# Load order, gate and slice order at the head of a fused attention and gated feed-forward kernel

## The chip, the core and the metric

The kernel runs on one NeuronCore of a Trainium2 chip. The metric is the device time of one execution in microseconds (us). Before the change it is 227.95 us, the median of three runs (227.84 to 228.86).

The core's engines run side by side, each through its own list of instructions in order: TensorE (PE) multiplies matrices, VectorE (DVE), ScalarE (ACT) and GpSimd (POOL) do elementwise work, and SyncE (SP) mostly issues transfers. Sixteen DMA engines carry all transfers, whichever engine issued them. PE writes its results to PSUM, which has eight banks here named b0 to b7.

## The reference

For each of 8 batches and 8 heads there are 512 rows x (64 wide) and 32 state rows. Both sides attend to each other, and what comes out goes through a feed-forward layer with a ReLU gate.

```python
def _attn_ref(x, state):                      # x (8, 8, 512, 64), state (8, 8, 32, 64)
    scores = scale * np.matmul(x, state.transpose(0, 1, 3, 2))
    ...                                       # softmax over the 32 state rows -> a
    xread = np.matmul(a, state)
    scores2 = scale * np.matmul(state, x.transpose(0, 1, 3, 2))
    ...                                       # softmax over the 512 x rows -> a2
    sread = np.matmul(a2, x)
    return np.concatenate([xread, sread], axis=2)

def _moe_ref(x, w_gate, w_val, w_out):        # x (4352, 512), d_ff 1536
    gate = np.maximum(x @ w_gate, 0.0)
    val = x @ w_val
    return gate * val @ w_out
```

The kernel doesn't form `xread`. For each batch it multiplies the state with the weights first (U = state @ w, the "c" and "u" units below), and then the softmaxed scores with U (the "gv" units), so a gv unit needs both the batch's attention (`ANS`) and a slice of `U`.

## The kernel before

The parts that the change touches. `x_dma_cast` loads a batch of x through GpSimd's queue, casting from float32 to bfloat16 on the way; the loads of batch 0 go through the queues of SyncE and ScalarE in float32, in four pairs of heads.

```python
    def x_dma_cast(b, parts=1):

        cast_on_load.add(b)
        xb_alloc(b)
        v = xb[b].rearrange("p (h c d) -> p h c d", h=H, c=NC)
        for i in range(parts):
            hs = slice(H * i // parts, H * (i + 1) // parts)
            nc.gpsimd.dma_start(out=v[:, hs], in_=x[b, hs].rearrange("h (p c) d -> p h c d", c=NC))
        xb[b] = xb[b].rearrange("p (h c d) -> p c h d", h=H, c=NC)

    def w_dma(src, dst, lo, hi):
        nc.gpsimd.dma_start(out=dst[:, :, lo:hi],
                            in_=src.rearrange("(j p) f -> p j f", p=128)[:, :, lo:hi])

    def wo_dma(lo, hi):
        nc.gpsimd.dma_start(out=wo_sb[:, lo:hi],
                            in_=moe_w_out.rearrange("(f p) m -> p f m", p=128)[:, lo:hi])
...
    def state_conv(g, half, eng):
        dst, src, keep = st_b[:, g % 3, :, half], st_f[:, g], odd[:, half:half + 1]
        if eng == "act":
            nc.scalar.activation(out=dst, in_=src, func=AF.Copy, scale=keep)
        else:
            e = {"dve": nc.vector, "pool": nc.gpsimd}[eng]
            e.tensor_scalar(out=dst, in0=src, scalar1=keep, scalar2=None, op0=ALU.mult)

    def state_T(g):
        ps = held["st", g] = bank("stT_ps").bitcast(BF16)[:, 0:512]
        for i in range(4):
            nc.tensor.transpose(ps.rearrange("p (q i m) -> p q i m", i=4, m=8)[:, :, i],
                                st_b[:, g % 3, i].rearrange("p h d -> p (h d)"), id128)

    def state_out(g, eng):
        copy[eng](out=stT[:, 2 * g:2 * g + 2].rearrange("p b j m -> p (b j m)"), in_=held["st", g])

...
            for c in range(NC):
                for h2 in range(2):
                    nc.tensor.transpose(ps[64 * h2:64 * h2 + 64, c, j], xb[b][:, c, 4 * half + 2 * j + h2], id128)
...
    def att_sum(b, jp):
        e_v = by_pair(e_sn[b], jp).rearrange("p r (j n) -> p r j n", n=Ns)
        cs = small.tile([128, 2 * NC, 2], FP32, name="cs", tag="cs")
        nc.vector.reduce_sum(out=cs, in_=e_v, axis=AX.X)
        rc = held["rc", b, jp] = small.tile([128, 2 * NC, 2], FP32, name="rc", tag="rc")
        nc.vector.reciprocal(out=rc, in_=cs)

    def att_scale(b, jp, eng="dve"):
        e_v = by_pair(e_sn[b], jp).rearrange("p r (j n) -> p r j n", n=Ns)
        {"dve": nc.vector, "pool": nc.gpsimd}[eng].tensor_tensor(out=by_pair(a_sn[b], jp).rearrange("p r (j n) -> p r j n", n=Ns), in0=e_v,
                                in1=held["rc", b, jp].to_broadcast([128, 2 * NC, 2, Ns]), op=ALU.mult)
...
    def u_mm(dst, b, w, lo, n):

        wsb = (wg_sb, wv_sb)[w]
        for j in range(NJ):
            for parity in range(2):
                r = 64 * parity
                nc.tensor.matmul(dst[parity][32 * j:32 * j + 32], stT[r:r + 64, b, j, 32 * parity:32 * parity + 32],
                                 wsb[r:r + 64, j, lo:lo + n], start=True, stop=True)
...
    def gv(b, jf):
        if b not in hsb:
            hsb[b] = hpool.tile([128, NF, S], BF16, name="h_sb", tag="h_sb")
        held["gv", b, jf] = [bank("gv_ps"), bank("gv_ps")], hsb[b][:, jf], S
        for w in range(2):
            for kc in range(NK):
                gv_mm(held["gv", b, jf][0], b, jf, w, kc)
```

`state_conv` makes the state bfloat16 for the transpose (`state_T`). `att_scale` divides the exponentials by their sums; its engine is an argument. A c unit multiplies the state with a slice of both weights, 128 or 256 columns wide; a u unit with 512 columns of one weight. A gv unit is four matmuls of 512 columns.

The opening, in the order in which it is issued:

```python
    ctx.enter_context(tc.manual_schedule())
    nc.vector.memset(warm, 0.0)
    xf[0] = xin.tile([128, H, NC, D], FP32, name="xf", tag="xf")
    for eng, j in ((nc.sync, 0), (nc.scalar, None), (nc.sync, 2), (nc.scalar, 1), (nc.scalar, 3)):
        if j is None:
            state_dma(eng, 0, 2)
        else:
            src = x[0, 2 * j:2 * j + 2].rearrange("h (p c) d -> p h c d", c=NC)
            eng.dma_start(out=xf[0][:, 2 * j:2 * j + 2], in_=src)
    make_identity(nc, id128)
    x_dma_cast(1, 2)
    nc.scalar.activation(out=tiny, in_=nc.const_aps.tensor(0.0, (128, 1), FP32), func=AF.Exp)
    nc.vector.reduce_sum(out=odd, in_=id128.rearrange("p (a h m) -> p h a m", h=2, m=8), axis=AX.XY)
    nc.gpsimd.memset(xa[:, :, :, D:D + 1], 1.0)

    def w_load(lo, n):
        w_dma(moe_w_gate, wg_sb, lo, lo + n)
        w_dma(moe_w_val, wv_sb, lo, lo + n)

    def late_loads():
        x_dma_cast(2)
        state_dma(nc.gpsimd, 2, B)
        wo_dma(0, 6)
        wo_dma(6, NF)
        x_dma(3, (nc.gpsimd,))

    def x_next(b):
        x_conv(b, 0, "pool")
        x_conv(b, 1, "pool")
        x_trans_dma(b)

    warm_ps = psum.tile([128, 512], FP32, name="warm_ps", tag="b7")

    def spin(n, cols=512):
        for i in range(n):
            nc.tensor.matmul(warm_ps[:, 0:cols], warm[:, 0:128], warm[:, 0:cols], start=True, stop=True)
```

`spin` is filler: matmuls on zeros whose results nobody reads, which keep PE busy while it would wait. The program that follows is a list of words, each a step with its arguments; the digits after @ are PSUM banks. Each engine runs its own words in this order. The steps that count here: `xc` casts a head pair of batch 0, `xT` and `xT2` transpose x on PE, `xo` copies the transposes out, `stc`, `stT`, `sto` do the same for the state, `sc` are the scores, `ex` the exponentials, `nr` their sums, `nx` the scaling, `aT` and `ao` transpose the attention and copy it out, `c`/`co`, `u`/`uo`, `gv` with `re` (ReLU) and `mu` (product), `o`/`of` the output product, `sr`/`sn` the state's side, `xp` a padded copy of x, `xn` the cast of the next batch, `wd` and `ld` the loads.

```python
    program = """
    stc.0.0.dve stc.0.1.act xc.0.0.pool spin.30.128 xT.0.0@0 stT.0@1 xc.0.1.pool wd.0.128 wd.128.128 wd.256.256
    wd.512.256 wd.768.256 wd.1024.256 wd.1280.256 ld xo.0.0.act xc.0.2.dve sto.0.act spin.10.128 xT.0.1@2 xo.0.1.dve
    xc.0.3.act spin.11.128 sc.0.0@3 xT.0.3@4 ex.0.0 xT.0.2@5 xo.0.3.dve xo.0.2.act nr.0.0 spin.14.128 sc.0.1@0
    xT2.1.0@1 ex.0.1 nx.0.0 xo2.1.0.act nr.0.1 spin.7.128 xT2.1.1@2 xo2.1.1.act spin.4.128 sc.1.0@3 nx.0.1 spin.7.128
    c.0.0.128@45 ex.1.0 sc.1.1@0 co.0.0.128.0.dve aT.0.0@1 co.0.0.128.1.act aT.0.1@2 nr.1.0 ex.1.1 ao.0.1.act
    spin.9.128 c.0.128.128@34 ao.0.0.dve c.1.128.128@50 co.0.128.128.0.act nr.1.1 spin.5.128 gv.0.0@21
    co.0.128.128.1.act co.1.128.128.1.act co.1.128.128.0.act nx.1.0 re.0.0 c.1.0.128@34 gv.0.1@05 nx.1.1
    co.1.0.128.1.act co.1.0.128.0.act mu.0.0 re.0.1 c.0.256.256@24 co.0.256.256.1.act co.0.256.256.0.dve
    ...
    mu.1.1 re.1.5 gv.1.0@02 mu.1.5 re.1.0 c.0.1024.256@54 mu.1.0 gv.1.4@31 co.0.1024.256.0.act co.0.1024.256.1.act
    gv.1.6@02 re.1.4 re.1.6 mu.1.4 gv.0.8@54 mu.1.6 re.0.8 gv.0.9@30 mu.0.8 stc.1.0.pool re.0.9 c.0.1280.256@15
    stc.1.1.pool stc.2.0.pool stc.2.1.pool stc.3.0.pool stc.3.1.pool xp.0 xp.1 xn.3 c.0.768.256@24 mu.0.9
    co.0.1280.256.1.act xT2.2.0@3 co.0.768.256.1.act co.0.1280.256.0.dve xT2.2.1@0 co.0.768.256.0.act xo2.2.0.dve
    stT.1@5 gv.0.10@41 sto.1.act xo2.2.1.dve re.0.10 gv.0.11@23 mu.0.10 re.0.11 gv.1.7@50 mu.0.11 re.1.7 sc.2.0@4
    gv.0.6@12 mu.1.7 ex.2.0 re.0.6 nr.2.0 gv.0.7@35 re.0.7 mu.0.6 o.0.0@6 mu.0.7 c.1.1280.256@40 u.2.0.0@13 nx.2.0
    ...
    aT.2.1@1 aT.2.0@4 ao.2.1.dve u.2.1.0@25 u.2.1.512@03 ao.2.0.dve uo.2.1.0.1.act sr.1@1 uo.2.1.0.0.dve o.0.7
    uo.2.1.512.0.act sn.1 uo.2.1.512.1.dve gv.2.2@45 re.2.2 gv.1.11@20 mu.2.2 re.1.11 gv.2.1@13 mu.1.11 re.2.1
    gv.2.3@45 mu.2.1 re.2.3 o.0.8 mu.2.3 gv.2.0@20 of.0.2.act re.2.0 o.0.9@7 mu.2.0 sr.0@1 sn.0 xp.2 xp.3
    """
```

After the program, a loop with a fixed pattern goes on from unit (2, 4) to the last batch; the change leaves it as it is.

The softmax here doesn't subtract the row's maximum and nothing guards it: scores larger than these inputs give would overflow.

## Time and profile before

| | |
|---|---|
| Median time | 227.95 us |
| Span in the profile | 226.6 us, granted PE clock 1.00 |
| ACT busy, DVE busy, POOL busy | 55%, 58%, 22% |
| PE idle, 60 to 212 us | 1.29 us of 152 |
| PE idle, 15 to 60 us | 1.32 us of 45 |
| PE idle, after 212 us | 3.55 us |
| Slices of weight loads landed | 11.30 to 27.73 us |

How to read it: a line of the groups or of the instructions in order of time names an engine, the line of the kernel (L117), the operation, what it writes and reads (out<-in), the shape and the count. In the order of time the first two numbers are the start and the duration in us, and the brackets at the end give the idle time of the engine just before and what ended it. "<-DMA" means that the landing of that transfer ended the wait. In the groups the numbers after the bar are the busy time in us, the mean of one instruction in ns, and the idle time before them. In the view of DMA issues the last number is the time from issue to landing in us, and the number of KB is counted in what is written.

### The profile page before, as it was taken

How to read it: one execution, taken by the hardware profiler on the slowest of the kernel's cores; microseconds unless marked ns; L12 is line 12 of the kernel's file. 1: busy time of each engine (PE TensorE's matmuls, PEld its weight loads, DVE VectorE, ACT ScalarE, POOL GpSimd, SP SyncE). 2: the span in 40 equal slices, each digit the busy share in tenths (PEclk: the TensorE clock that was granted, in tenths of full speed). 3: DMA queues.
4: the chain of work that ended last, by engine and by line, in shares of the span. 5: the costliest groups of instructions: out<-in, count | busy, mean ns of one | idle time of the engine just before them, and what ended most of it. 6: DMA issues, size and time to landing. Idle time of an engine off the chain costs nothing.

```text
span 226.6 us, 4970 instructions
## 1 busy us (share of the span) xinstructions
PE 219.1 (97%) x2004; PEld 110.8 (49%) x2033; DVE 130.4 (58%) x228; ACT 125.1 (55%) x238; POOL 49.6 (22%) x54
## 2 busy tenths in 40 slices
PE   7999999999999999999999999999999999999994
PEld 7764354444444444444434444345443444666543
DVE  1588777976488547764776468656755343222100
ACT  4698886745475754664556555455655444322221
POOL 6975349500643060006000600000000000000000
PEclk9999999999999999999999999999999999999999
DMA  6999999180718911591139213611311111111132
GB/s 207 170 160 196 197 243 273 53 185 0 227 53 123 293 53 46 123 283 61 48 87 246 91 46 93 142 46 46 95 46 49 48 46 48 48 49 67 72 94 94
DMA packets 37816, 25.76 MB, mean 114 GB/s; under 512 B 18880, under 2 KB 33216, under 8 KB 37792
## 3 DMA queue, kind: packets, MB, share of 16 engines
q1 hardware_dynamic: 25184, 17.11, 27.1%
q0 software_dynamic: 11440, 7.21, 20.6%
q10 hardware_dynamic: 1168, 1.11, 1.7%
...
## 4 chain that ended last, share of the span: by engine, by line
PE 92%; DMA 3%; issue 1%; DVE 1%; ACT 1%; POOL 0%; ACTq 0%; DVEq 0%; POOLq 0%
PE o_ps L347 37%; PE gv_ps L310 37%; PE gv_ps L327 5%; PE up L285 4%; DMA xf<-in_x_dram 3%; PE sc_ps L206 2%; PE upc L285 1%; PE sr_ps L258 1%; PE warm_ps L424 1%; PE o_ps L373 1%; DVE h_sb L338 1%; PE xT_ps L192 1%; PE aT_ps L241 0%; POOL st_b L135 0%; PE srT_ps L271 0%
## 5 line engine op out<-in xcount | busy, mean ns | idle before, releaser
L310 PE MATMUL gv_ps<-ans,U 128*128 128x512 bf16 x365 | 95.4, 380 | 1.3 <-DVE sn L267 0.3
L347 PE MATMUL o_ps<-wo_sb,h_sb 128*128 128x512 bf16 x362 | 93.6, 379 | 0.9 <-issue 0.3
L338 DVE TENSOR_TENSOR h_sb<-gv_ps,g_sb 128x512 bf16<-128x512 f32 x96 | 65.0, 687 | 42.0 <-ACT g_sb L334 40.0
L334 ACT ACTIVATE g_sb<-gv_ps 128x512 bf16<-128x512 f32 (+1 forms) x108 | 63.0, 584 | 45.9 <-PE gv_ps L310 33.2
L347 PEld LDWEIGHTS <-h_sb 128*128 128x128 bf16 x372 | 36.1, 98 | 41.2 <-issue 0.5
L310 PEld LDWEIGHTS <-U 128*128 128x128 bf16 x384 | 34.9, 98 | 41.2 <-issue 4.5
L355 ACT COPY o_sb<-o_ps 128x512 f32<-128x512 f32 x31 | 18.1, 585 | 21.7 <-PE o_ps L347 21.7
L295 DVE CAST U<-up 128x512 bf16<-128x512 f32 x37 | 23.9, 685 | 5.6 <-PE up L285 5.5
L295 ACT CAST U<-up 128x512 bf16<-128x512 f32 x35 | 18.9, 593 | 10.5 <-PE up L285 10.5
L153 POOL CAST xb<-xf 128x1024 bf16<-128x1024 f32 (+1 forms) x12 | 11.8, 1007 | 52.2 <-DMA xf<-in_x_dram 41.9
L250 POOL COPY xa<-xb 128x2048 bf16<-128x2048 bf16 x8 | 15.0, 1894 | 17.1 <-issue 14.1
L219 DVE TENSOR_REDUCE cs<-e_sn 128x16 f32<-128x512 bf16 x16 | 10.9, 682 | 8.4 <-ACT e_sn L213 8.4
L338 DVE TENSOR_TENSOR hs_sb<-gv_ps,g_sb 128x256 bf16<-128x256 f32 x12 | 5.1, 425 | 15.3 <-PE gv_ps L327 10.5
L225 DVE TENSOR_TENSOR a_sn<-e_sn,rc 128x512 bf16<-128x512 bf16 x16 | 12.5, 784 | 0.4
L213 ACT ACTIVATE e_sn<-sc_ps 128x512 bf16<-128x512 f32 x16 | 9.6, 601 | 5.1 <-PE sc_ps L206 4.9
L305 ACT CAST U<-upc 128x512 bf16<-128x512 f32 (+1 forms) x21 | 9.9, 522 | 2.1 <-PE upc L285 1.9
L285 PEld LDWEIGHTS <-stT 64*32 64x32 bf16 x512 | 5.0, 89 | 10.8 <-issue 10.1
L424 PE MATMUL warm_ps<-hs_sb 128*128 128x128 bf16 x97 | 9.0, 258 | 1.2 <-DVE hs_sb L390 1.2
L424 PEld LDWEIGHTS <-hs_sb 128*128 128x128 bf16 x97 | 7.6, 119 | 1.5 <-DVE hs_sb L390 1.2
L206 PEld LDWEIGHTS <-xT 128*128 128x128 bf16 x128 | 5.7, 98 | 3.4 <-DVE xT L183 0.4
L285 PE MATMUL up<-wg_sb,stT 64*32 64x512 bf16 x144 | 7.4, 386 | 0.0
L327 PE MATMUL gv_ps<-br,wg_sb 128*128 128x256 bf16 x48 | 7.2, 273 | 0.1
...
## 6 DMA issues: line engine op xcount, KB each, us to landing
out_dram<-o_sb SPq DMA_DIRECT2D x31, 256.0 KB, 2.3
xf<-in_x_dram SPq DMA_DIRECT2D x4, 1024.0 KB, 6.5
...
wg_sb<-in_moe_w_gate_dram POOLq DMA_DIRECT2D x5, 256.0 KB, 9.1
wv_sb<-in_moe_w_val_dram POOLq DMA_DIRECT2D x5, 256.0 KB, 9.6
xf<-in_x_dram POOLq DMA_DIRECT2D x1, 1024.0 KB, 18.0
xf<-in_x_dram SPq DMA_DIRECT2D x2, 256.0 KB, 4.3
xf<-in_x_dram ACTq DMA_DIRECT2D x2, 256.0 KB, 5.2
```

The costliest lines, as they stand in the source:

```text
L153: copy[eng](out=xb[b][:, :, hs].rearrange("p c h d -> p h c d"), in_=xf[b][:, hs])
L225: {"dve": nc.vector, "pool": nc.gpsimd}[eng].tensor_tensor(out=by_pair(a_sn[b], jp).rearrange("p r (j n) -> p r j n", n=Ns), in0=e_v, in1= ...
L250: nc.gpsimd.tensor_copy(out=v.rearrange("p c h d -> p h c d"), in_=xb[b].rearrange("p c h d -> p h c d"))
L285: nc.tensor.matmul(dst[parity][32 * j:32 * j + 32], stT[r:r + 64, b, j, 32 * parity:32 * parity + 32], wsb[r:r + 64, j, lo:lo + n], start= ...
L295: copy[eng](out=U[b][:, w, kc, lo:lo + 512], in_=held["u", b, w, lo][kc])
L310: nc.tensor.matmul(ps[w], U[b][:, w, kc, f0:f0 + 128], ANS[b][:, kc].rearrange("p c t -> p (c t)"), start=(kc == 0), stop=(kc == NK - 1))
L327: nc.tensor.matmul(ps[w][:, 0:nt], wsb[:, j, f0:f0 + 128], br[:, j].rearrange("p b n -> p (b n)"), start=(j == 0), stop=(j == NJ - 1))
L334: nc.scalar.activation(out=g_sb[:, 0:n], in_=ps[0][:, 0:n], func=AF.Relu)
L338: nc.vector.tensor_tensor(out=dst, in0=ps[1][:, 0:n], in1=held["g", b, jf][:, 0:n], op=ALU.mult)
L347: nc.tensor.matmul(held["o", b, tsub], src[:, jf, tsub * 128:(tsub + 1) * 128], wo_sb[:, jf], start=(jf == 0), stop=(jf == NF - 1))
L355: copy[eng](out=o_sb, in_=held["o", b, tsub])
L424: nc.tensor.matmul(warm_ps[:, 0:cols], warm[:, 0:128], warm[:, 0:cols], start=True, stop=True)
```

## The change

GpSimd's queue carries most of the loads. Until now its first load was issued at once, beside batch 0's loads on the other two queues. With the change GpSimd first copies one column of batch 0's first head pair into a scratch tile (`gate`), so that its queue begins only when that pair has landed. The weight loads are no longer in one block: each is a word of the program (`dw`, `dx`, `ds`, `do`, `df`), placed among GpSimd's other words. GpSimd no longer casts the first two head pairs of batch 0, and it does half of the scaling (`nx`) of batches 0 and 1 and all of that of batch 2. The padded copies `xp.0` and `xp.1` go ahead of the conversion of the state. The order of the weight slices and of the gv units between them is new, and so is the number of spins: 88 in place of 97. The set of PE units is the same.

It is for getting batch 0's attention, and with it the first gv unit, going earlier, by keeping the DMA engines free for batch 0's x at the start.

```diff
@@ -107,16 +107,6 @@
 
     cast_on_load = set()
 
-    def x_dma_cast(b, parts=1):
-
-        cast_on_load.add(b)
-        xb_alloc(b)
-        v = xb[b].rearrange("p (h c d) -> p h c d", h=H, c=NC)
-        for i in range(parts):
-            hs = slice(H * i // parts, H * (i + 1) // parts)
-            nc.gpsimd.dma_start(out=v[:, hs], in_=x[b, hs].rearrange("h (p c) d -> p h c d", c=NC))
-        xb[b] = xb[b].rearrange("p (h c d) -> p c h d", h=H, c=NC)
-
     def w_dma(src, dst, lo, hi):
         nc.gpsimd.dma_start(out=dst[:, :, lo:hi],
                             in_=src.rearrange("(j p) f -> p j f", p=128)[:, :, lo:hi])
@@ -396,21 +386,22 @@
             src = x[0, 2 * j:2 * j + 2].rearrange("h (p c) d -> p h c d", c=NC)
             eng.dma_start(out=xf[0][:, 2 * j:2 * j + 2], in_=src)
     make_identity(nc, id128)
-    x_dma_cast(1, 2)
+    nc.gpsimd.memset(xa[:, :, :, D:D + 1], 1.0)
+    nc.gpsimd.tensor_copy(out=gate, in_=xf[0][:, 0, 0, 0:1])
     nc.scalar.activation(out=tiny, in_=nc.const_aps.tensor(0.0, (128, 1), FP32), func=AF.Exp)
     nc.vector.reduce_sum(out=odd, in_=id128.rearrange("p (a h m) -> p h a m", h=2, m=8), axis=AX.XY)
-    nc.gpsimd.memset(xa[:, :, :, D:D + 1], 1.0)
-
-    def w_load(lo, n):
-        w_dma(moe_w_gate, wg_sb, lo, lo + n)
-        w_dma(moe_w_val, wv_sb, lo, lo + n)
-
-    def late_loads():
-        x_dma_cast(2)
-        state_dma(nc.gpsimd, 2, B)
-        wo_dma(0, 6)
-        wo_dma(6, NF)
-        x_dma(3, (nc.gpsimd,))
+
+    def w_load(w, lo, n):
+        w_dma((moe_w_gate, moe_w_val)[w], (wg_sb, wv_sb)[w], lo, lo + n)
+
+    def x_load(b, part, parts):
+        if part == 0:
+            cast_on_load.add(b)
+            xb_alloc(b)
+            xb[b] = xb[b].rearrange("p (h c d) -> p c h d", h=H, c=NC)
+        hs = slice(H * part // parts, H * (part + 1) // parts)
+        nc.gpsimd.dma_start(out=xb[b][:, :, hs].rearrange("p c h d -> p h c d"),
+                            in_=x[b, hs].rearrange("h (p c) d -> p h c d", c=NC))
 
     def x_next(b):
         x_conv(b, 0, "pool")
@@ -425,36 +416,39 @@
 
 
 
-    steps = {"spin": spin, "stc": state_conv, "stT": state_T, "sto": state_out, "xc": x_conv_pair, "xT": x_T, "xT2": x_T2, "xo2": x_out2, "wd": w_load, "ld": late_loads, "xo": x_out,
+    steps = {"spin": spin, "stc": state_conv, "stT": state_T, "sto": state_out, "xc": x_conv_pair, "xT": x_T, "xT2": x_T2, "xo2": x_out2, "dw": w_load, "dx": x_load, "ds": lambda: state_dma(nc.gpsimd, 2, B), "do": wo_dma,
+             "df": lambda b: x_dma(b, (nc.gpsimd,)), "xo": x_out,
              "sc": att_sc, "ex": att_exp, "nr": att_sum, "nx": att_scale, "aT": att_T, "ao": att_out,
              "c": c_unit, "co": c_out, "u": u_unit, "uo": u_out, "gv": gv, "re": relu, "mu": mult, "o": out_part,
              "of": fin_x, "xn": x_next, "xp": x_pad, "sr": sr_mm, "sn": sr_norm}
     program = """
... (the removed lines of the program, which stand in the kernel above)
+    stc.0.0.act stc.0.1.act xc.0.0.dve dx.1.0.2 spin.28.128 xT.0.0@0 stT.0@1 xo.0.0.dve dx.1.1.2 sto.0.act xc.0.1.dve
+    xc.0.2.act dw.0.0.128 spin.14.128 xT.0.1@2 xc.0.3.dve xo.0.1.act spin.3.128 xT.0.2@3 dw.1.0.128 xT.0.3@4
+    xo.0.2.act sc.0.0@5 xo.0.3.dve dw.0.128.128 ex.0.0 spin.6.128 sc.0.1@0 dw.1.128.128 nr.0.0 ex.0.1 spin.7.128
+    xT2.1.0@1 dw.0.256.256 nr.0.1 xo2.1.0.act nx.0.0.pool spin.14.128 xT2.1.1@2 nx.0.1 sc.1.0@3 dw.1.256.256
+    xo2.1.1.dve ex.1.0 spin.3.128 aT.0.1@4 ao.0.1.act spin.3.128 c.0.0.128@50 dw.0.512.256 nr.1.0 aT.0.0@1 sc.1.1@3
+    co.0.0.128.0.act co.0.0.128.1.act c.1.0.128@24 dw.1.512.256 ao.0.0.dve ex.1.1 co.1.0.128.0.dve spin.10.128
+    c.0.128.128@50 co.1.0.128.1.act dw.0.768.256 nr.1.1 gv.0.0@13 co.0.128.128.1.act co.0.128.128.0.act nx.1.0.pool
+    re.0.0 gv.0.1@24 nx.1.1 re.0.1 mu.0.0 dw.1.768.256 c.1.128.128@05 aT.1.1@1 co.1.128.128.1.act mu.0.1 aT.1.0@2
+    dw.0.1024.256 co.1.128.128.0.act c.0.256.256@35 ao.1.0.act ao.1.1.dve c.1.256.256@04 dw.1.1024.256
+    co.0.256.256.1.dve co.0.256.256.0.act gv.1.1@12 co.1.256.256.0.act co.1.256.256.1.dve dw.0.1280.256 re.1.1
+    gv.0.3@35 dw.1.1280.256 mu.1.1 re.0.3 gv.0.2@04 dx.2.0.1 mu.0.3 re.0.2 c.1.512.256@13 ds mu.0.2 gv.1.0@25
+    co.1.512.256.1.act do.0.6 co.1.512.256.0.act c.0.512.256@04 re.1.0 gv.1.4@31 co.0.512.256.0.dve do.6.12
+    co.0.512.256.1.act mu.1.0 re.1.4 gv.1.2@20 xp.1 mu.1.4 re.1.2 gv.0.5@43 mu.1.2 re.0.5 c.0.768.256@51 xp.0 mu.0.5
+    gv.1.3@20 co.0.768.256.0.act co.0.768.256.1.act c.1.1024.256@43 re.1.3 gv.0.7@51 co.1.1024.256.1.dve
+    co.1.1024.256.0.act df.3 mu.1.3 re.0.7 gv.1.5@23 mu.0.7 re.1.5 gv.1.8@45 mu.1.5 re.1.8 gv.0.6@01 mu.1.8 re.0.6
+    c.0.1024.256@23 c.0.1280.256@45 mu.0.6 co.0.1024.256.1.act xT2.2.0@0 co.0.1280.256.0.act co.0.1280.256.1.dve
+    xT2.2.1@1 stc.1.0.pool xo2.2.0.act stc.1.1.pool gv.0.4@34 xo2.2.1.dve stc.2.0.pool co.0.1024.256.0.act
+    stc.2.1.pool stT.1@5 stc.3.0.pool gv.1.9@01 re.0.4 sto.1.dve stc.3.1.pool re.1.9 mu.0.4 sc.2.1@2 gv.0.8@53 mu.1.9
+    ex.2.1 re.0.8 nr.2.1 gv.0.10@04 re.0.10 mu.0.8 gv.0.11@21 nx.2.1.pool mu.0.10 re.0.11 gv.0.9@50 mu.0.11 re.0.9
+    sc.2.0@3 o.0.0@6 mu.0.9 ex.2.0 nr.2.0 u.2.1.1024@24 c.1.768.256@15 uo.2.1.1024.1.act c.1.1280.256@30 o.0.1
+    co.1.768.256.0.dve uo.2.1.1024.0.act nx.2.0.pool co.1.1280.256.0.dve co.1.768.256.1.act o.0.2 co.1.1280.256.1.dve
+    aT.2.0@4 of.0.0.dve gv.1.6@12 xn.3 ao.2.0.dve re.1.6 o.0.3@7 mu.1.6 u.2.1.512@53 u.2.0.512@04 uo.2.1.512.0.act
+    uo.2.1.512.1.dve u.2.0.1024@12 o.0.4 uo.2.0.1024.0.act uo.2.0.512.0.dve uo.2.0.1024.1.act o.0.5 uo.2.0.512.1.dve
+    o.0.6@6 of.0.1.dve u.2.1.0@53 u.2.0.0@10 uo.2.1.0.0.act uo.2.1.0.1.dve sr.1@2 o.0.7 uo.2.0.0.1.act sn.1
+    uo.2.0.0.0.dve gv.1.11@45 re.1.11 aT.2.1@3 gv.1.7@02 mu.1.11 ao.2.1.act re.1.7 gv.2.1@14 mu.1.7 re.2.1 gv.2.0@35
+    mu.2.1 re.2.0 o.0.8 mu.2.0 gv.1.10@02 of.0.2.dve re.1.10 gv.2.3@14 mu.1.10 re.2.3 gv.2.2@35 mu.2.3 re.2.2 o.0.9@7
+    mu.2.2 sr.0@0 sn.0 xp.2 xp.3
     """
     for word in program.split():
         word, _, banks = word.partition("@")
```

## Prediction

> **What bounds the kernel now.** I read the page's busy line and its chain first. TensorE (PE) is busy for 219.1 of 226.6 us and carries 92% of the chain, so only its idle time and its useless work can be won.
>
> ```profile
> PE 219.1 (97%) x2004; PEld 110.8 (49%) x2033; DVE 130.4 (58%) x228; ACT 125.1 (55%) x238; POOL 49.6 (22%) x54
> PE 92%; DMA 3%; issue 1%; DVE 1%; ACT 1%; POOL 0%; ACTq 0%; DVEq 0%; POOLq 0%
> L424 PE MATMUL warm_ps<-hs_sb 128*128 128x128 bf16 x97 | 9.0, 258 | 1.2 <-DVE hs_sb L390 1.2
> ```
>
> The last line is the useless work: 97 filler matmuls (`spin`), all of them before the first gate/value unit. The busy time by stretches then says where PE is not full: it is idle for 7.5 us in all, of which 1.2 us lies before the first instruction and 3.55 us after 212 us, which the change does not touch. From 60 to 212 us only 1.29 us is idle, again untouched. Between 15 and 60 us it is 1.32 us. So the change can act on some 8 us of spins, some 0.6 us of gaps before 14.8 us, and 1.3 us later.
>
> Next the instructions in order of time, for the head and for the place where PE waits later on:
>
> ```profile
> 1.42 1.71 POOL L117 DMA_DIRECT2D xb<-in_x_dram  x2
> 3.83 0.61 POOL L153 CAST xb<-xf 128x512 bf16<-128x512 f32 x1 [0.30 <-DMA xf<-in_x_dram]
> 7.72 0.62 ACT L153 CAST xb<-xf 128x512 bf16<-128x512 f32 x1 [1.51 <-DMA xf<-in_x_dram]
> 11.78 0.69 DVE L225 TENSOR_TENSOR a_sn<-e_sn,rc 128x512 bf16<-128x512 bf16 x1
> 14.78 1.03 PE L310 MATMUL gv_ps<-ans,U 128*128 128x512 bf16 x3
> ...
> 31.59 2.73 POOL L135 TENSOR_SCALAR st_b<-st_f,odd 128x256 bf16<-128x256 f32 x3 [6.70 <-DMA st_f<-in_state_dram]
> 33.48 0.40 PE L140 MATMUL stT_ps<-id,st_b 128*128 128x128 bf16 x4 [0.27 <-POOL st_b L135]
> ```
>
> Batch 0's head pairs land at 3.77, 5.51, 6.89 and 7.70 us; the first gv unit starts at 14.78. And at 33.48 PE waits for GpSimd (POOL), which has itself waited 6.70 us for the state of batches 2 to 7. That second wait matters more than its 0.27 us suggests. A look at the load issues by small windows gives that load's flight time, and GpSimd's own order shows how it got its place:
>
> ```profile
> 19.99 0.75 POOL L96 DMA_DIRECT2D st_f<-in_state_dram  x1 [0.45 <-DMA wv_sb<-in_moe_w_val_dram]
> ```
> ```profile
> st_f<-in_state_dram POOLq DMA_DIRECT2D x1, 384.0 KB, 11.4
> ```
>
> From 16 us on each of GpSimd's issues waits for the landing of the load eight places ahead (here a wv slice, landed 19.71), and loads land back to back: the trace's 256 KB weight slices at 15.73, 17.03, 18.38, 19.71 ... 27.73, one each 1.3 us, then x of batch 2 at 30.39, the state at 31.41, the two halves of w_out at 35.13 and 39.06, x of batch 3 at 41.99. The DMA engines are thus a second bound of the first 40 us, running just ahead of PE: c.0.256 uses its wv slice at 17.07, 0.04 us after it landed.
>
> **What the Trainium skill says.** "GPSIMD Engine Reference", 3.1 Elementwise: a two-input tensor_tensor costs GpSimd about 2.6 cycles per element (at 1.2 GHz) against one on VectorE. My estimate from that for 512 elements is 1.1 us plus dispatch, say 1.3. The trace before has no such instruction; its one-input TENSOR_SCALAR of only 256 elements takes 912 ns, so up to 2 us is possible. "SBUF — State Buffer", Who interferes with whom: a VectorE instruction with two SBUF inputs blocks against a GpSimd one that reads SBUF. The trace agrees: the scaling of batch 2 took 1.64 us at 39.60, under GpSimd's copy of xa, and 0.68 at 47.07 without. "TensorE: Matmul & The Clock Gate", What's actually happening: PE runs at half clock until it has been busy for about 3.4 us. The trace agrees in kind: 30 spins take 3.3 us (110 ns each), those from 6.65 to 7.26 55 ns each. "DMA: Bandwidth & Descriptors", Queues, rings and completion order: each DMA engine takes turns between queues, packet by packet. Here the trace says otherwise: batch 1's x was issued at 1.42, but its first packet moved at 5.16 us, on the engine that had just finished its hardware-queue work, 5.14 us.
>
> **The change part by part.**
>
> *Gate.* GpSimd's first load now waits for the first head pair (3.77 us), so it begins near 3.95, not 1.42. From the packet records this frees little. Most DMA engines finish batch 0's x at 5.14 to 5.48 in the kernel before, with batch 1 standing behind it anyway. Only a few lag (6.42 for pair 2, 7.34 for pair 3), and these share with batch 1 at the end: some 11 packets of 60 ns, 0.7 us. So pair 3 lands near 7.0 instead of 7.7, the others as before. Issue to first packet took at most 1.8 us for the first weight slice (6.12 to 7.9), so batch 1 starts near 5.75 instead of 5.16 on the free engines. The laggards, which set each landing, never run dry, so batch 1's x should land at about 9.2 and 10.6 again and the weights as before, or up to 0.5 us later, or earlier by the 0.47 us by which w_gate's first slice is now issued (5.65 against 6.12: GpSimd has two 0.61 us casts fewer).
>
> *Scaling on GpSimd.* nx.0.0 and nx.1.0 leave VectorE (0.69 and 0.61 us) and cost GpSimd about 1.3 us each between issues. The load queue then holds four slices or more (over 4 us of transfer), and from 16 us issues wait for landings anyway: nothing lost, some 0.5 us of VectorE won.
>
> *Slice order up to the first gv.* The same PE units stand before gv.0.0 (3 c units of 128, 4 sc, 4+2 transposes of x, 2 aT), with 88 spins instead of 97: 9 x 0.06 = 0.5 us less. Walking the chain with the durations above: pair 3 cast on DVE 7.05 to 7.5, xT.0.3 to 7.95, sc.0.0 to 8.5, exps 8.7 to 9.9 (ACT has two copies ahead of them), sums to 10.3 and 11.3, nx.0.0 on GpSimd 10.3 to 11.6, nx.0.1 to 12.1, aT.0.1 12.3, c.0.0 (its slices landed 12.02), aT.0.0, sc.1.1, c.1.0 to 13.4, ten spins 0.6, c.0.128 and gv.0.0 at 14.2. Gain 0.6 us.
>
> *From there to stT.1.* The number of units ahead of stT.1 is equal: 15 gv, 8 c of 256, all else. Now c.0.256 comes after gv.0.1, c.1.128 and both aT.1: 14.2 + 1.73 + 0.2 + 0.54 = 16.7, and its wv slice lands at 17.03: 0.3 us of the gain is lost there, but the 0.29 us wait for a copy of U at 18.18 goes, as aT.1 is done. Fifteen gv of 0.864, the c units of 0.35 and the rest bring PE to stT.1 at about 32.5, against 33.2 before. There it needs the state: landing 31.41, then two GpSimd passes of 0.91, so 33.4 at the earliest. **The gain of 0.7 us ends in a longer wait at stT.1**, since state's load keeps its place in the queue (x of 2, state, w_out, x of 3), and nothing in the change shortens the bytes ahead of it.
>
> *After stT.1.* Equal units again (13 gv, 10 o, 2 c, 6 u, 2 sc, 2 aT, 2 sr), about 24.0 us of work in 24.5 us. xa's copies go ahead of state (23.5 to 27.3 us, while GpSimd would wait), nx.2 leaves VectorE and its 1.64 us: perhaps 0.2 us of the 0.5 is won. x of batch 3 is issued near 28 instead of 24.0 but its place in the queue is the same, 42 us.
>
> Sum: 0.6 won at the head, 0.1 in the middle, 0.7 given back at stT.1 less the 0.27 that was lost there already (arrival 33.2, start 33.48, now 33.4), 0.2 won later: 227.95 - 0.1 - 0.2 = 227.65 us.
>
> **Rivals.** (1) The loads come sooner: with no mixing at the start batch 1 and the early weights land 0.5 to 1 us earlier, stT.1 too, and the whole head gain survives: 226.6 to 227.0. For it: packet rates between 11 and 16 us are below the later steady rate (about 320 against 384 per us), so there is slack. Against it: every DMA engine is busy from 5.2 us in the kernel before. (2) The gate leaves the DMA engines idle: if the first software load needs as long as the 3.7 us seen from issue to first packet, batch 1 begins at 7.7, all loads slip by 1 us or more, c.0.256 and stT.1 with them: 228.7 to 229.5. Against: w_gate's first slice was moving 1.8 us after its issue. (3) GpSimd's scaling takes 2 us or more and blocks VectorE's half beside it: gv.0.0 at 14.8, no head gain, and still stT.1 at 33.4: 227.8. (4) The new order meets a bank or a copy late after stT.1: 0.5 to 1 us slower; the many changes of engine per copy speak for some of this.
>
> **Range and chances.** All these lie within -1.4 and +1.5 us of before; 2% is 4.6 us, and that would take nearly half of all the spins and gaps the change can reach (8 + 0.6 + 1.3), or a stall that no rival makes. Range 226.6 to 228.9. Faster by over 2%: 0.01; slower: 0.02.
>
> **What would show it.** In the changed profile: pair 3's cast near 7 us; x of batch 1 landing near 9.2 and 10.6; TENSOR_TENSOR of 128x512 on POOL at 1.2 to 2 us; first gv at 14.2 (13.7 to 14.8); the state landing at 31.4 and a PE wait of 0.5 to 1 us on `st_b` at stT.1, starting again near 33.4. I am wrong if state lands 0.7 us or more to either side, or if PE finds a new wait after it.

## The result, and the profile after

The changed kernel takes 229.80 us (median of 4 runs, 229.63 to 229.96), beside 228.18 us for the kernel before on the same chip: a ratio of 1.0067 [1.0041, 1.0093] (95% interval). A longer comparison later gave 229.54 us (18 executions) beside 228.09 us (39): 1.0063 [1.0046, 1.0080]. So the change costs about 1.5 us, where a gain of 0.3 us was predicted, and the time lies above the range that was given. Single executions of one kernel differ by about 1 us, so medians decide here, and a profile is one execution out of them.

The page of the kernel after, its busy line, its chain and the spins:

```profile
PE 218.0 (96%) x1995; PEld 109.3 (48%) x2024; DVE 131.2 (57%) x229; ACT 123.7 (54%) x235; POOL 52.4 (23%) x57
...
PE 82%; DMA 10%; POOL 4%; issue 1%; DVE 0%; DVEq 0%
...
L415 PE MATMUL warm_ps<-hs_sb 128*128 128x128 bf16 x88 | 7.8, 249 | 1.2 <-DVE hs_sb L380 1.2
```

Nine matmuls fewer, as planned (2004 to 1995), and 1.1 us less busy time on PE. Yet the span grew from 226.6 to 228.2 us, so PE's idle time grew by 2.7 us. The chain says where to look first: transfers now carry 10% of it (3% before) and GpSimd 4% (0% before), PE 82% in place of 92%.

The instructions of the kernel after in order of time (start, duration, then what it is, and in brackets the idle time just before and what ended it), from the opening to the state's transpose:

```profile
4.30 0.44 POOL L390 COPY gate<-xf 128x1 f32<-128x1 f32 x1 [2.69 <-DMA xf<-in_x_dram]
4.68 1.78 POOL L403 DMA_DIRECT2D xb<-in_x_dram  x2
...
6.49 0.43 DVE L143 CAST xb<-xf 128x512 bf16<-128x512 f32 x1 [0.33 <-DMA xf<-in_x_dram]
...
10.16 1.09 POOL L215 TENSOR_TENSOR a_sn<-e_sn,rc 128x512 bf16<-128x512 bf16 x1
...
10.19 1.62 DVE L215 TENSOR_TENSOR a_sn<-e_sn,rc 128x512 bf16<-128x512 bf16 x1
...
11.38 0.64 PE L182 MATMUL xT_ps<-id,xb 128*64 128x128 bf16 x16 [1.15 <-DMA xb<-in_x_dram]
...
14.09 0.25 PE L275 MATMUL upc<-wv_sb,stT 64*32 64x128 bf16 x8 [0.99 <-DMA wv_sb<-in_moe_w_val_dram]
...
15.97 1.90 PE L300 MATMUL gv_ps<-ans,U 128*128 128x512 bf16 x7
...
32.54 3.63 POOL L125 TENSOR_SCALAR st_b<-st_f,odd 128x256 bf16<-128x256 f32 x4 [3.45 <-DMA st_f<-in_state_dram]
...
34.43 0.40 PE L130 MATMUL stT_ps<-id,st_b 128*128 128x128 bf16 x4 [0.16 <-POOL st_b L125]
```

The last head pair of batch 0 is in at 6.46 us (7.70 before), and its cast runs at 6.49, as the gate was to bring about. (no_gate below shows that the gate is not what does it in this order.) But the loads behind the gate come later: the second half of batch 1's x lands at 11.34 us (10.58 before) and PE waits 1.15 us for it; w_val's first slice makes PE wait 0.99 us; the first gv unit starts at 15.97 us, not at 14.2. The state lands at 32.45 us (31.41 before), and its transpose starts at 34.43, 0.95 us later than before. A second profile of the same kernel has gv.0.0 at 14.94 and the transpose at 34.28: the head scatters, the state's place hardly moves between these two. In four edited kernels below that keep the gate the transpose starts at 33.47 to 33.60 us, though an edit like that of sr0_bank2, one digit at the end of the program, can't reach it: executions differ by up to 1 us here too.

At the end of the program text there is a second difference. The kernel before, in order of time, at `sr.0` (the product on bank 1) and the loop's first gv unit:

```profile
57.59 0.43 PE L258 MATMUL sr_ps<-xa,e_sn 128*32 128x65 bf16 x32
...
57.96 0.39 PE L310 MATMUL gv_ps<-ans,U 128*128 128x512 bf16 x1
...
58.30 0.29 DVE L267 TENSOR_TENSOR sn<-sr_ps,rr 128x128 bf16<-128x128 f32 x1
...
58.65 0.60 PE L310 MATMUL gv_ps<-ans,U 128*128 128x512 bf16 x2 [0.30 <-DVE sn L267]
```

and the kernel after:

```profile
58.32 0.43 PE L248 MATMUL sr_ps<-xa,e_sn 128*32 128x65 bf16 x32
...
59.02 0.29 DVE L257 TENSOR_TENSOR sn<-sr_ps,rr 128x128 bf16<-128x128 f32 x1
...
59.37 1.04 PE L300 MATMUL gv_ps<-ans,U 128*128 128x512 bf16 x3 [0.62 <-DVE sn L257]
```

Before, PE starts on the gv unit 0.37 us after the start of `sr.0`, and waits 0.30 us ahead of its second bank. After, it waits 0.62 us ahead of the first, until VectorE has read the product.

The third difference lies at the very end. The view of the DMA issues of the kernel before from 219.7 to 225 us, with the fetch of PE's instructions as a queue of its own (packets, MB, share) and the outputs (count, KB, us from issue to landing):

```profile
q8 instruction: 1, 0.02, 1.4%
...
out_dram<-o_sb SPq DMA_DIRECT2D x1, 256.0 KB, 2.1
...
out_dram<-o_sb ACTq DMA_DIRECT2D x1, 128.0 KB, 1.9
```

and that of the kernel after from 220.6 to 226 us:

```profile
q8 instruction: 1, 0.02, 1.7%
...
out_dram<-o_sb SPq DMA_DIRECT2D x1, 256.0 KB, 4.1
...
out_dram<-o_sb ACTq DMA_DIRECT2D x1, 128.0 KB, 3.2
```

The same outputs take 2.0 and 1.3 us longer to land. From the start of the last PE matmul to the last landing it was 2.28 us (223.23 to 225.51) and is 2.89 (224.13 to 227.02). The fetch holds up outputs in both kernels. Before, it comes at 220.53 us, and the two outputs issued at 219.22 and 219.27 take 3.57 and 3.68 us, where the same two take 1.77 and 1.95 us in the kernel after; but these are not the last ones. After, it comes at 223.46 us and meets the last.

By stages, profile after against profile before: up to the state's transpose +0.95 us; from there to `sr.0` -0.22; `sr.0` to the first gv unit +0.68; from there to the last PE matmul -0.51, of which 0.30 is the wait that the kernel before has there; from that to the last landing +0.61. That makes the 1.51 us between the last landings (225.51 and 227.02). Two profiles can't tell which of these are the change's and which are scatter. The experiments can.

### The profile page after: what moved, and what is told of

Read it like the earlier page. It is cut to its first block, busy times and chain, and to the rows that moved or that the text cites. A ratio compares the mean times of both kernels' runs of the same rounds, so it can differ in the third digit from the quotient of the medians.

```text
span 228.2 us, 4958 instructions
## 1 busy us (share of the span) xinstructions
PE 218.0 (96%) x1995; PEld 109.3 (48%) x2024; DVE 131.2 (57%) x229; ACT 123.7 (54%) x235; POOL 52.4 (23%) x57
## 4 chain that ended last, share of the span: by engine, by line
PE 82%; DMA 10%; POOL 4%; issue 1%; DVE 0%; DVEq 0%
PE o_ps L337 38%; PE gv_ps L300 31%; DMA st_f<-in_state_dram 5%; PE gv_ps L317 5%; PE up L275 4%; DMA wv_sb<-in_moe_w_val_dram 4%; DMA xf<-in_x_dram 2%; POOL wg_sb L111 1%; PE sr_ps L248 1%; PE sc_ps L196 1%; PE o_ps L363 1%; POOL wv_sb L111 1%; POOL st_b L125 1%; POOL xb L403 1%; POOL a_sn L215 0%
## 5 line engine op out<-in xcount | busy, mean ns | idle before, releaser
L345 ACT COPY o_sb<-o_ps 128x512 f32<-128x512 f32 x28 | 16.4, 585 | 19.8 <-PE o_ps L337 19.8
L285 ACT CAST U<-up 128x512 bf16<-128x512 f32 x37 | 19.9, 592 | 13.0 <-PE up L275 13.0
L285 DVE CAST U<-up 128x512 bf16<-128x512 f32 x35 | 22.6, 686 | 6.3 <-PE up L275 6.2
L143 POOL CAST xb<-xf 128x1024 bf16<-128x1024 f32 x10 | 10.1, 1040 | 48.0 <-DMA xf<-in_x_dram 38.2
L295 ACT CAST U<-upc 128x512 bf16<-128x512 f32 (+1 forms) x19 | 9.1, 518 | 2.0 <-PE upc L275 1.9
L215 DVE TENSOR_TENSOR a_sn<-e_sn,rc 128x512 bf16<-128x512 bf16 x12 | 9.2, 770 | 0.5
L415 PE MATMUL warm_ps<-hs_sb 128*128 128x128 bf16 x88 | 7.8, 249 | 1.2 <-DVE hs_sb L380 1.2
L275 PE MATMUL up<-wv_sb,stT 64*32 64x512 bf16 x144 | 7.2, 378 | 0.0
L317 PE MATMUL gv_ps<-br,wv_sb 128*128 128x256 bf16 x48 | 7.2, 273 | 0.0
```

What stands on the lines that cost most here:

```text
L143: copy[eng](out=xb[b][:, :, hs].rearrange("p c h d -> p h c d"), in_=xf[b][:, hs])
L285: copy[eng](out=U[b][:, w, kc, lo:lo + 512], in_=held["u", b, w, lo][kc])
L317: nc.tensor.matmul(ps[w][:, 0:nt], wsb[:, j, f0:f0 + 128], br[:, j].rearrange("p b n -> p (b n)"), start=(j == 0), stop=(j == NJ - 1))
L345: copy[eng](out=o_sb, in_=held["o", b, tsub])
```

## The experiments

The theory after the first look: three costs that have nothing to do with each other. The gate delays the whole stream of loads; the bank digit of `sr.0` makes the loop's first unit wait; and with 18 PE instructions fewer (9 spins, each a matmul and a weight load) the last fetch of PE's instructions falls into the last outputs. The rivals: the gate alone costs everything, and the rest follows from the later start; GpSimd's scaling holds its load issues up; the nine spins are missed for PE's clock and not for the fetch.

All twelve runs, in three groups of four rows, each on a chip of its own and beside the kernel before (228.14, 228.09 and 228.20 us). Where rows of two groups are compared, the kernel before is the bridge; its medians differ by 0.11 us at most.

| Kernel | Median us | To the kernel before |
|---|---|---|
| no_gate | 228.88 | 1.0027 [1.0011, 1.0043] |
| sr0_bank2 | 228.80 | 1.0030 [1.0014, 1.0045] |
| pe_pad | 228.92 | 1.0038 [1.0025, 1.0051] |
| nx_dve | 229.46 | 1.0051 [1.0029, 1.0073] |
| after_again | 229.54 | 1.0063 [1.0046, 1.0080] |
| mix | 227.50 | 0.9972 [0.9957, 0.9987] |
| before_less9 | 230.57 | 1.0099 [1.0066, 1.0132] |
| before_gate | 230.15 | 1.0082 [1.0052, 1.0112] |
| mix_gate | 228.27 | 0.9998 [0.9986, 1.0010] |
| mix_88 | 228.04 | 0.9986 [0.9964, 1.0008] |
| mix_ds | 226.97 | 0.9944 [0.9927, 0.9961] |
| mix_ds_spin | 228.05 | 0.9992 [0.9970, 1.0015] |

A difference between two of these medians is uncertain by about 0.5 us (half intervals of 0.0017 and 0.0014 of 228 us are 0.39 and 0.32 us; the root of the sum of their squares is 0.50).

**no_gate**: the changed kernel, its loads not held back.

```diff
-    nc.gpsimd.tensor_copy(out=gate, in_=xf[0][:, 0, 0, 0:1])
```

> Changed kernel without the one-column copy that makes GpSimd wait for batch 0's first head pair, all else as changed. Gate theory (the whole load stream starts 1 us late and stays late): batch 1's x lands near 9.2 and 10.6, the state near 31.4 instead of 32.45, stT.1 starts at 33.4 to 33.6 instead of 34.43, and the time falls by 0.8 to 1.0 us to 228.8 to 229.0. Rival (the loads are late because GpSimd scales between the issues, or by chance): the state still lands after 32 us and the time stays within 0.3 us of 229.8.

Measured: 228.88 us, 0.66 below the 229.54 of the changed kernel. GpSimd in order of time:

```profile
1.45 1.74 POOL L402 DMA_DIRECT2D xb<-in_x_dram  x2
...
31.42 5.43 POOL L125 TENSOR_SCALAR st_b<-st_f,odd 128x256 bf16<-128x256 f32 x6 [3.47 <-DMA st_f<-in_state_dram]
```

The first load is issued at 1.45 us and not at 4.68, and the state's conversion starts at 31.42, not at 32.54 (32.39 in the second profile of the changed kernel). The three kernels sr0_bank2, pe_pad and nx_dve, which keep the gate, have the conversion at 31.57 to 31.72 too, so this profile alone would prove little; the time does. With one instruction nearly half of what the change loses is gone; the rest isn't, so the gate is not the whole of it.

The DMA engines' busy share from 5.4 to 6.6 us, in tenths over 40 slices, for the changed kernel and for no_gate:

```profile
DMA  9999999995534021210000000000000012216146
```
```profile
DMA  9898999999999999999999999999999999999999
```

Behind the gate the engines run dry when batch 0 is through, and from 5.97 to 6.36 us nothing moves at all. And the last head pair lands at 6.42 us without the gate as well, and at 6.33 to 6.37 in mix, mix_88 and mix_ds (7.68 in mix_ds_spin). So in this order the gate doesn't bring batch 0 in sooner; what else in the change does isn't tested.

**sr0_bank2**: one digit, so that the loop's first gv unit finds its banks free.

```diff
-    mu.2.2 sr.0@0 sn.0 xp.2 xp.3
+    mu.2.2 sr.0@2 sn.0 xp.2 xp.3
```

> Changed kernel with sr.0 in PSUM bank 2 instead of 0, one digit. Bank theory (the loop's first gv unit takes banks 0 and 1, and its first pair waits 0.62 us for sn.0 to read bank 0; in the kernel before sr.0 stood in bank 1 and only the second pair waited): the wait of gv on sn is gone and the time falls by 0.5 to 0.65 us to 229.2 to 229.3. Rival (the wait is slack that the next wait for VectorE or ScalarE takes up): the wait moves to a later unit and the time falls by less than 0.2 us.

Measured: 228.80 us, 0.74 below, more than was expected. In order of time:

```profile
57.35 0.43 PE L248 MATMUL sr_ps<-xa,e_sn 128*32 128x65 bf16 x32
...
57.72 1.04 PE L300 MATMUL gv_ps<-ans,U 128*128 128x512 bf16 x4
...
58.05 0.29 DVE L257 TENSOR_TENSOR sn<-sr_ps,rr 128x128 bf16<-128x128 f32 x1
```

All four matmuls of the unit run 0.37 us after the start of `sr.0`, ahead of VectorE's read. The profile shows 0.68 us won against the changed kernel (1.05 to 0.37, the same in every profile with either digit), and the time agrees.

**pe_pad**: nine spins more, put where PE waits for batch 1's x, so that PE has as many instructions as in the kernel before.

```diff
-    xT2.1.0@1 dw.0.256.256 nr.0.1 xo2.1.0.act nx.0.0.pool spin.14.128 xT2.1.1@2 nx.0.1 sc.1.0@3 dw.1.256.256
+    xT2.1.0@1 dw.0.256.256 nr.0.1 xo2.1.0.act nx.0.0.pool spin.23.128 xT2.1.1@2 nx.0.1 sc.1.0@3 dw.1.256.256
```

> Changed kernel with 9 more spins (97 as before) in the 1.15 us wait for batch 1's second half, where they cost nothing. Fetch theory (PE's instruction stream is loaded in 16 KB pieces by one DMA engine; with 18 PE instructions fewer the last piece moves some 2 us later and falls on the last output transfers, which then take 4.1 us in place of 2.1): the last piece is loaded before 223 us, the last landing comes 1.6 to 1.7 us after PE's last matmul instead of 2.3, and the time falls by 0.5 to 0.7 us to 229.1 to 229.3. Rival (the late landing at the end is chance or has another cause): the time stays within 0.15 us of 229.8 and the last outputs are as late.

Measured: 228.92 us, 0.62 below, by adding work that nobody reads. Its DMA issues from 219.5 to 225 us:

```profile
q8 instruction: 1, 0.02, 1.7%
...
out_dram<-o_sb SPq DMA_DIRECT2D x1, 256.0 KB, 2.1
```

The outputs are as quick as in the kernel before. The last fetch runs at 220.00 us, 3.19 us ahead of the last PE matmul; in the changed kernel it was at 223.46, 0.67 us ahead. The end from that matmul to the last landing is 2.29 us again.

**nx_dve**: the scaling of batch 0 and 1 wholly on VectorE.

```diff
-nx.0.0.pool
+nx.0.0.dve
...
-nx.1.0.pool
+nx.1.0.dve
```

> Changed kernel with the scaling of batches 0 and 1 (nx.0.0, nx.1.0) on VectorE again. Gate theory: GpSimd's scaling is beside the loads, so the loads land as in the changed kernel to 0.3 us, gv.0.0 starts within 0.3 us of 15.97 and the time stays within 0.25 us of 229.8. Rival (the scaling holds up the issue of the weight slices by 1.1 us each time, and blocks VectorE's half, 1.62 us instead of 0.69): the slices from the fifth on and the state land 0.5 to 1 us earlier, and the time falls by 0.5 us or more.

Measured: 229.46 us, 0.08 below the changed kernel, which is nothing. VectorE then does both halves, in 1.22 us together at 10.27, and GpSimd's share neither helps nor harms. In this profile the state lands at 31.62 us, 0.8 us ahead of 32.45, which was the rival's sign, and gv.0.0 starts at 14.56 and not near 15.97. But in sr0_bank2, pe_pad and mix_gate, with the scaling on GpSimd, the state lands at 31.48 to 31.60 as well, and the time did not fall. The rival of load issues held up by the scaling falls by the time.

**after_again** and **mix**: the changed kernel once more in the same group, and the three edits of no_gate, sr0_bank2 and pe_pad together.

> The changed kernel itself, unedited, for a second profile and more times beside the edits (single executions scatter by about 1 us). If its first profile was typical, the state lands near 32.45 and stT.1 starts near 34.4. If, as four edited kernels that still have GpSimd's scaling or the gate suggest, that profile had unusually late loads, the state lands at 31.4 to 31.8, stT.1 starts at 33.4 to 33.7, gv.0.0 at 14.4 to 15.0, and what is lost lies at sr.0's bank (0.4 us) and after PE's last matmul (0.6 to 1.0 us). Time 229.3 to 229.8.

> Changed kernel without the gate, with sr.0 in bank 2 and with 97 spins: the three edits that each saved 0.6 to 0.9 us. If they are separate costs they add up: 227.1 to 227.5, below the kernel before (228.14). Rival (each single edit only moved the same last piece of PE's instructions off the last outputs, so the savings overlap): 228.4 to 228.8.

Measured: 229.54 and 227.50 us, so 2.04 us for the three together. One by one they gave 0.66 + 0.74 + 0.62 = 2.02 us. Had one cost been the cause of another, the sum would be larger than what they give together; they add up, though the comparison of sum and whole is itself uncertain by about 1 us. The rival's 228.4 to 228.8 us is out. What is left of the change is 0.28% faster than the kernel before. PE's waits in the first 62 us of after_again (who waits, for what, us in total, times, longest):

```profile
PE xT_ps L182 <- DMA xb<-in_x_dram: 1.0, 1, 1.0
PE stT_ps L130 <- POOL st_b L125: 0.9, 1, 0.9
PE gv_ps L300 <- DVE sn L257: 0.6, 1, 0.6
```

and of mix:

```profile
PE xT_ps L169 <- DVE xb L143: 0.6, 1, 0.6
PE stT_ps L130 <- POOL st_b L125: 0.5, 1, 0.5
...
PE upc L275 <- issue: 0.3, 1, 0.3
```

The waits for batch 1's x and for `sn` are gone, and a shorter one for the state stays. A new one of 0.6 us is for the first head pair of batch 0. The pair doesn't come late, at 4.11 us (4.25 and 4.07 in the two profiles of the changed kernel); but VectorE's cast of it, beside GpSimd's load issues, takes 0.79 us there and 0.73 and 0.76 in no_gate and mix_ds, where behind the gate it takes 0.43. (It takes 0.43 in mix_88 and mix_ds_spin too.) The line with "issue" is a gap of PE inside a c unit, where nothing is awaited; all five kernels of this order without the gate have one, of 0.25 to 0.53 us.

**before_less9**: the kernel before with nine spins fewer, to have the fetch alone from its side.

```diff
-spin.30.128 xT.0.0@0
+spin.21.128 xT.0.0@0
```

> Kernel before with 21 instead of 30 spins at the start, where PE waits for x anyway: 18 PE instructions fewer, as in the changed kernel. Fetch theory: the last 16 KB piece of PE's instructions moves from 220.5 to about 222.5 us, the last landing comes 3 us or more after PE's last matmul begins instead of 2.3, and the time rises by 0.6 to 1.0 us to 228.8 to 229.1. Rival: the end is as before and the time is within 0.25 us of 228.14.

Measured: 230.57 us, 2.5 us above the kernel before: far more than the fetch costs elsewhere. The last fetch did move, to 224.25 us, 0.73 ahead of the last PE matmul, and the end is 2.90 us long. But the spins were taken from the first ones, the filler that brings PE to its full clock: eleven spins from 7.08 us took 1.38 us, where eleven from 6.65 us took 0.78 in the kernel before, and the full rate came only at about 9.5 us. And in its order of time stands the longest gap of this kind in any profile:

```profile
16.95 0.45 PE L424 MATMUL warm_ps<-hs_sb 128*128 128x128 bf16 x5 [1.67 <-issue]
```

The gap falls inside a run of spins, where nothing is awaited. A fetch of PE's instructions began at 14.72 us and took 0.94 us, while loads kept the DMA engines busy at 90% or more. That PE waited for its instructions is inferred from this order: here and in the five kernels with the shorter gap PE goes on 1.3 to 1.6 us after such a fetch has ended. Three things moved at once, so this run says nothing on the size of the fetch at the end. It does show that the number of spins moves more than one place.

**before_gate**: the kernel before with the gate alone.

```diff
+    nc.gpsimd.memset(xa[:, :, :, D:D + 1], 1.0)
+    nc.gpsimd.tensor_copy(out=gate, in_=xf[0][:, 0, 0, 0:1])
     x_dma_cast(1, 2)
     ...
-    nc.gpsimd.memset(xa[:, :, :, D:D + 1], 1.0)
```

> Kernel before with the gate alone: GpSimd's first load waits for batch 0's first head pair. My reading of the four runs: batch 1's first packet moves 1 us later (6.2), but its landings and the weights' slip by 0.3 us or less on most executions, since a late weight slice only costs where PE waits: time up by 0 to 0.4 us to 228.1 to 228.5. Rival (the gate delays the whole stream): state lands 0.8 us or more after 31.41, time up by 0.7 to 1 us.

Measured: 230.15 us, 2.06 above the kernel before. In this order the gate does bring the last head pair in sooner, at 6.28 us against 7.70. The state lands at 32.98 us, 1.57 later than before, which was the rival's sign. But the gate's price is not read cleanly from it either, since the kernel before casts the first two head pairs on GpSimd, and these casts now stand behind the gate and two load issues. PE in order of time:

```profile
6.62 0.40 PE L179 MATMUL xT_ps<-id,xb 128*128 128x128 bf16 x4 [2.26 <-POOL xb L153]
```

That is a reason to move these casts off GpSimd together with the gate, as the change does.

**mix_gate** and **mix_88**: one cost put back into mix at a time, the gate or the 88 spins.

```diff
+    nc.gpsimd.tensor_copy(out=gate, in_=xf[0][:, 0, 0, 0:1])
```
```diff
-    ... nx.0.0.pool spin.23.128 xT2.1.1@2 ...
+    ... nx.0.0.pool spin.14.128 xT2.1.1@2 ...
```

> The three-edit kernel with the gate back in: changed kernel with sr.0 in bank 2 and 97 spins. It measures the gate where nothing else is amiss. If the gate costs what its single removal saved (0.66 us): 228.1 to 228.3 against 227.5. If that removal saved by chance: within 0.25 us of 227.5.

> The three-edit kernel with 88 spins again (no gate, sr.0 in bank 2). Fetch theory, other direction: the last 16 KB piece of PE's instructions moves from 219.5 to 221.5 us or later, the last landing comes 3 us or more after the start of PE's last matmul instead of 2.3, time 228.0 to 228.3. Rival (the end of the changed kernel was late for another reason): within 0.2 us of 227.5.

Measured: 228.27 us, 0.77 above mix, and 228.04, 0.54 above mix. The first is clear of the uncertainty of a difference (here 0.44 us); the second isn't by itself (0.6 us), but its profile shows the end as the theory has it. The profiles of mix and mix_gate, both of executions near 227.8 us, end within 0.09 us of each other, so where the gate's 0.77 us arises they don't show. The DMA issues of mix_88 from 217.9 to 224 us:

```profile
q8 instruction: 1, 0.02, 1.0%
...
out_dram<-o_sb SPq DMA_DIRECT2D x1, 256.0 KB, 4.6
```

In that execution the head went well: the state's transpose at 32.41 us, 1.26 earlier than in the profile of mix, and the last PE matmul at 221.43, 1.27 earlier. The last landing came at 224.85, only 0.13 earlier. So 1.1 us of a better head was lost in the last outputs. The spins missing elsewhere can't explain that: up to the last matmul this execution is the quicker one.

**mix_ds**: mix, with the state's load issued ahead of batch 2's x. If the wait for the state is what ends the head's gain, this is where the gain comes back.

```diff
-    gv.0.3@35 dw.1.1280.256 mu.1.1 re.0.3 gv.0.2@04 dx.2.0.1 mu.0.3 re.0.2 c.1.512.256@13 ds mu.0.2 gv.1.0@25
+    gv.0.3@35 dw.1.1280.256 mu.1.1 re.0.3 gv.0.2@04 ds mu.0.3 re.0.2 c.1.512.256@13 dx.2.0.1 mu.0.2 gv.1.0@25
```

> The three-edit kernel with the state's load issued ahead of batch 2's x instead of behind it. The step of the prediction that a gain at the head ends in a wait for the state at stT.1: the state lands near 29 instead of 31.7, x of batch 2 near 30.7 instead of 30.7 to 31.7, PE no longer waits at stT.1 (0.48 us now), time 227.0 to 227.2. Rival (PE is held just after by the next load, w_out or batch 2's x): the wait moves and the time stays within 0.15 us of 227.5.

Measured: 226.97 us, 0.53 below mix (uncertain by 0.52 us), and 0.56% faster than the kernel before (0.9944 [0.9927, 0.9961]): it beats both kernels. In order of time:

```profile
28.67 5.43 POOL L125 TENSOR_SCALAR st_b<-st_f,odd 128x256 bf16<-128x256 f32 x6 [0.86 <-DMA st_f<-in_state_dram]
...
33.07 0.39 PE L130 MATMUL stT_ps<-id,st_b 128*128 128x128 bf16 x4
```

The state is in at 28.58 us, GpSimd's two passes are over long before 33, and the transpose has no wait ahead of it; batch 2's x lands at 31.09, which is early enough. Now PE alone sets the 33.07.

**mix_ds_spin**: mix_ds, with the ten spins ahead of c.0.128 taken out and six put in front.

```diff
-    ... xc.0.0.dve dx.1.0.2 spin.28.128 xT.0.0@0 ...
+    ... xc.0.0.dve dx.1.0.2 spin.34.128 xT.0.0@0 ...
-    ... co.1.0.128.0.dve spin.10.128
+    ... co.1.0.128.0.dve
```

> As the last one, and the ten spins ahead of c.0.128 are taken out, six put at the start where PE waits for x: gv.0.0 starts 0.5 to 0.6 us earlier (14.3), which only pays once the state is no longer awaited: 226.5 to 226.8. Rival (the weight slices are the next bound): c.0.256 or a later c unit waits for its slice and the time stays near that of the last one. 93 spins in all, so the last piece of PE's instructions comes near 220.5 and should miss the last outputs.

Measured: 228.05 us, 1.08 above mix_ds. Neither the gain nor the rival's wait for a weight slice came. Its profile is of the slowest of its 14 executions (229.52 us), so what it shows of the head need not hold for the median. There VectorE's cast of the last head pair starts at 7.70 us (in mix_ds it is over at 7.14), and PE waits for the load that was moved back:

```profile
32.52 1.08 PE L182 MATMUL xT_ps<-id,xb 128*64 128x128 bf16 x32 [0.91 <-DMA xb<-in_x_dram]
```

With 93 spins its last fetch falls at 222.64 us, and the end is 3.17 us long. How much of the 1.08 us is the fetch (about 0.6, by the runs above), and how much the head, this run doesn't tell.

## Why the prediction was wrong

The time stays within 2%, which had nearly all the chances, but it is 1.45 us above the kernel before (229.54 and 228.09) and was put 0.3 us below it. The three costs sum to 2.0 us; the kernel before already pays some 0.3 us of the bank's (its wait of 0.30 us at 58.65), which leaves 1.7 us of new cost. 1.7 less the predicted gain of 0.3 is 1.4 us, and 1.45 is measured. The range ended at 228.9 us, though Rival 2 of the same prediction went to 229.5; that the time came out there is chance, since the gate, which that rival is about, is 0.7 us of it.

**The gate: wrong, 0.7 us.** The step said that the laggards among the DMA engines never run dry, so that batch 1's x and the weights land as before. They do run dry: nothing moves from 5.97 to 6.36 us. Pair 3 did come early (6.46 us, 7.0 predicted), but so it did without the gate (6.42), and the stream of loads was late: the first packet behind the gate moved at 6.2 to 6.4 us in the gated kernels and at 5.4 to 5.5 in the ungated ones of the same order, where 5.75 was predicted. The gate opened later than assumed: its copy of one column took 0.44 us and the first issue stood at 4.68 us, not at 3.95; w_gate's first slice followed at 6.45, not at 5.65, and so later than before (6.12). Over the profiles of the changed order, the second half of batch 1 landed at 10.74 us on average with the gate and 9.69 without, the state at 31.83 and 31.15, and its transpose started at 33.81 and 33.13. The loss of 0.68 us at the transpose is near what the runs cost (0.66 and 0.77 us). But the three profiles without the gate have the transpose at 32.41 to 33.67 us and the six with it at 33.47 to 34.43: they overlap, so the cost is shown by time, and that it is lost through the loads is the likely way and not a proven one. Rival 2 had the mechanism, idle DMA engines and all loads slipping, with more than the runs show in size. Rival 1, loads that come sooner, has nothing for it. The kernel before had shown batch 1's first packet at 5.16 us, when batch 0's packets began to run out; those loads then stood ready, issued at 1.42 us. (The records name a packet's queue and not its DMA engine, so that it moved on an engine that had just become free is inferred.) Behind the gate the loads don't stand ready: 2.1 us go by from the pair's landing (4.25 us) to their first packet (6.37), and the engines are dry for the last part of it.

**Scaling on GpSimd: right, with a shorter instruction.** 1.05 to 1.10 us instead of the 1.3 that was taken. The Trainium skill's "GPSIMD Engine Reference", 3.1 Elementwise (2.6 cycles per element at 1.2 GHz, which makes my estimate for 512 elements 1.1 us) agrees without anything on top. VectorE's half beside it took 1.62 us in one profile and 1.23 in another, 0.69 alone, so the two do block each other as the prediction had it for the kernel before. By nx_dve that costs nothing. Rival 3 falls.

**Slice order up to the first gv: not seen.** gv.0.0 starts at 15.97 and 14.94 us in the two profiles of the changed kernel, and at 14.2 to 14.9 in the other profiles of its order bar mix_ds_spin; 14.2 was predicted and 14.78 was before. The walk rested on batch 1's x at 9.2 and 10.6 us and on weights at 12.02; PE's wait of 1.0 and 1.15 us for the former and 0.99 for the latter is the first step's error again. But it is not all of it: without the gate batch 1's x lands at 9.46 to 10.15 us, and gv.0.0 still starts at 14.83 to 14.92 in no_gate, mix and mix_ds (14.23 in mix_88). There the longer cast and PE's gap with nothing awaited, seen at mix, stand in its way.

**From there to stT.1: the mechanism right, shown by mix_ds.** The head's gain ends in the wait for the state. In four of six gated profiles the transpose starts at 33.47 to 33.60 us, 33.4 predicted, and in the two profiles of the changed kernel at 34.28 and 34.43, which is the state's landing, two passes of 0.91 us and some 0.15. Without that wait (mix_ds) 0.53 us is won, just clear of the uncertainty.

**After stT.1: the gain right, a loss overlooked.** "Equal units again" gave 0.2 us, and the profile has 0.22 from the transpose to `sr.0`. But the step didn't compare the bank digits of the last words with those of the loop behind them: `sr.0` moved from bank 1 to bank 0, and the loop's first unit, which the diff doesn't show, begins on bank 0. It costs 0.74 us by time, 0.68 by profile, of which 0.3 was there before on the second bank. Rival 4, a bank met late after stT.1, is this.

**What bounds the kernel: wrong at the end, 0.6 us.** "3.55 us after 212 us, which the change does not touch" failed. (The idle time there is 3.15 us: the stretch that was read ran 0.4 us past the end of the span.) Nothing that computes was touched; but PE's instructions come through the same DMA engines in pieces of 16 KB (16 packets, 0.26 MB on the page), and the last piece came at another place. With 97 spins it is fetched with 36 to 39 matmuls still to start, 2.7 to 3.3 us ahead of the last one; with 88 or 93 spins with 12 to 15 left, 0.65 to 0.83 us ahead (in mix_88 with none left, 0.33 us behind). All fourteen profiles fall in two groups by it: with the early fetch the end is 2.28 or 2.29 us long (before, pe_pad, mix, mix_gate, mix_ds, before_gate), with the late one 2.89 to 3.43 (the eight others). That the number of instructions costs 0.5 to 0.6 us through the last outputs is shown in both directions (0.62 and 0.54 us), with the uncertainty named above.

How the number of spins sets the place isn't shown. Nine spins are eighteen instructions, nine matmuls and their weight loads; a fetch that simply came that much later would move by nine matmuls, and it moved by more than twenty, with 93 spins as far as with 88. Nor is it shown how one packet holds up outputs by so much. The packet keeps one DMA engine for 1.22 us in the kernel before and 1.43 us in the changed one, while the 256 KB output lands 2.0 to 2.6 us later. In seven of the eight late profiles ScalarE's issue of its last output takes 0.84 to 1.42 us as well, in place of 0.36. The rival that the spins are missed for PE's clock falls for the changed kernel: in its profile 14 spins from 5.43 us take 0.94 us, which is the full rate, and the nine in pe_pad stand where PE waits, and the outputs' landing changed.

**Still open.** Why the DMA engines move only 276 and 277 packets per us from 8.2 to 10 us in the two profiles of the changed kernel, where it is 403 to 425 in the other four with the gate and 628 to 675 in the five without; why the loads of one kernel's executions differ by 1 us; and the gate's and the spins' price in the old order, for which both runs had a second effect.
